# Holding v by whole batch rows: 72 loads of up to nine chunks in place of 144 of one

## The chip, the cores and the metric

The kernel runs on one core of a Trainium2 chip. The metric is the time that the device takes for one execution, in microseconds (us). Runs are compared by their median. Besides the timed runs one execution is recorded by the hardware profiler; it has a time of its own and is the source of every row below.

## What is computed

Three stages follow one another. Attention is done inside chunks of 64 tokens; its output, 4608 rows of 512 numbers, goes through a mixture of eight experts with a skip (a row whose skip score isn't positive passes unchanged, the others go to the expert with the highest logit), and then through a layer that takes the maximum of three products and multiplies it by a fourth matrix. All arrays are float32.

```python
# q, k, v: (8 batches, 8 heads, 576 tokens, 64)
chunk = 64
nc = S // chunk                                   # 9 chunks in a batch
scores = scale * np.matmul(q_c, k_c.transpose(0, 1, 2, 4, 3))
attn = np.exp(scores - np.max(scores, axis=-1, keepdims=True))
attn = attn / (np.sum(attn, axis=-1, keepdims=True) + 1e-09)
x = np.matmul(attn, v_c)                          # then rows of 8 x 64 = 512, token by token
do_compute = x @ w_skip > 0
e_idx = np.argmax(x[do_compute] @ w_gate, axis=1)
y = gate_w[:, None] * (np.maximum(xc @ w1[e], 0.0) @ w2[e])   # for the rows of expert e
h = np.maximum(np.maximum(x @ m2_w1, x @ m2_w2), x @ m2_w3)
out = h @ m2_w_out
```

## The kernel before, in words

The 4608 tokens are walked in 36 tiles of 128 (two chunks each); two tiles make a unit of 256, of which there are 18. A batch has 576 tokens, nine chunks, so units and batches don't end together: `pieces(u)` (L191) gives the parts of a unit that lie in one batch.

`load_qk` (L201) loads q and k of a unit, 512 KB each, in rows of 512 bytes, one transfer for each part. `load_v` (L216) loads v of a unit, one transfer for each chunk and each parity of the heads: 64 tokens stand on 64 partitions (the lower 64 for even heads, the upper 64 for odd ones), four heads of 64 numbers each, so a transfer is 64 KB in pieces of 256 bytes. Eight transfers make a unit and 144 the whole of v. They go into four buffers `v_all` of four chunks each. A column of ones beside each head (L186) makes the matmul of L290 give the row sums too.

All these loads are issued by SP, in the order that the queue of SP has them in. At the start `in_turn` (L575) chains them: q and k of units 0 to 4, with v of units 0, 1 and 2 behind units 1, 2 and 3. Behind those stand two small loads (L590, L591) of the gate's and the skip's weights into `wcat`, 18 KB together. ACT casts `wcat` to `wr` (L592), and DVE writes the other half of `wr` (L593).

Then the loop of L597 runs over the tiles, and PE's instructions stay in the order in which the loop writes them (L596). At step t it does the products with v of tile t-2 (`values`, L283), the scores of tile t (`scores`, L252), the transposes of tile t-1's exponentials, the logits of the unit that ended before (`logits`, L328, the tile `lt` of L333, every second step, for the first time at step 4), the transposes of q and k of the next unit, and the transposes of tile t-2's output. `lt` reads `wr`. At every second step a unit of q and k is loaded ahead (five units) and one of v (three units). Each four tiles make a group; `route` and `place` work out where its rows go, POOL stores the group's rows to `x_dram` (L470) and sends the row numbers (L448).

From step 22 on the first expert's weights are loaded by SP too (L97). The experts start as the last tiles end, and the third stage follows them. None of them reads v.

DMAs that POOL issues are described in a scratch of SBUF; its size is an argument of the constructor (L1132), 16384 bytes of a partition if nothing is said.

Of the kernel before, what the change touches and what calls it, by code (L numbers as in the profile page):

```python
# [9 lines left out]
F32 = mybir.dt.float32  # L10
# [9 lines left out]
P = 128  # L20
B, H, S, D = 8, 8, 576, 64
# [7 lines left out]
NU = N // UT  # L29
# [8 lines left out]
def kernel(  # L38
# [15 lines left out]
    nc = tc.nc  # L54
# [16 lines left out]
    def four_kb(shape, dt, name, aside=False):  # L71
        return bpool.tile(shape, dt, tag="s4" if aside else "b4", name=name, bufs=2 if aside else 4)
# [103 lines left out]
    def two_banks(tag, name):  # L176
        return psum1.tile([P, 2, 512], F32, tag=tag, name=name)

    apool = p1.enter_context(tc.tile_pool(name="apool", bufs=2))
    nc.gpsimd.memset(ids_sb, N)  # L180
    nc.gpsimd.dma_start(ids_dram.rearrange("(p c) o -> p (c o)", p=P), ids_sb)

    NV = 4
    v_all = [apool.tile([P, 4, 4, D + 1], F32, name=f"v_all{i}", bufs=1) for i in range(NV)]
    for i, t in enumerate(v_all):
        (nc.gpsimd if i else nc.vector).memset(t[:, :, :, D], 1.0)  # L186
    none = kpool.tile([1, XW], F32, name="none")
# [3 lines left out]
    def pieces(u):  # L191
        got, t = [], u * UT
        while t < (u + 1) * UT:
            b, s = divmod(t, S)
            n = min((u + 1) * UT - t, S - s)
            got.append((t - u * UT, b, s, n))
            t += n
        return got
# [14 lines left out]
                        dst[pr, h0:h1], src[b, h0:h1, s:s + n, :].rearrange("h (p r) d -> p h (r d)", r=2))  # L213
        units[u] = {"qt": qt, "kt": kt}

    def load_v(u):  # L216
        vb = v_all[u % NV]
        for off, b, s, n in pieces(u):
            for c in range(n // 64):
                for par in range(2):  # L220
                    link["load"] = nc.sync.dma_start(
                        vb[64 * par:64 * par + 64, off // 64 + c, :, :D],
                        v[b, par::2, s + 64 * c:s + 64 * c + 64, :].rearrange("hp k d -> k hp d"),
                    )

    def pair_heads(u, g):
        un = units[u]
        for nm in ("q", "k"):
            r = apool.tile([P, 2, H // 2, D], F32, tag=nm + "r", name=f"{nm}r{u}_{g}", bufs=3)
            (nc.scalar.copy if u == 0 else nc.gpsimd.tensor_copy if nm == "q" and u > 1 else nc.vector.tensor_copy)(  # L230
                r, un[nm + "t"][:, 4 * g:4 * g + 4, :].rearrange("p h (r d) -> p r h d", r=2))
            un[nm + "r", g] = r

    def qk_transpose(u, g):
        un = units[u]
        if g == 0:
            for nm in ("qT", "kT"):
                un[nm] = apool.tile([P, 4, UT], F32, tag=nm, name=f"{nm}{u}")
        for nm in ("q", "k"):
            src, dst = un[nm + "r", g], un[nm + "T"]  # L240
            tr = ps_tr(f"tr{nm}{u}_{g}").rearrange("p (h r t) -> p h r t", h=2, r=2)
            for hh in range(2):
                hp = 2 * g + hh
                for r in range(2):
                    nc.tensor.transpose(
                        tr[:, hh, r, :], src[:, r, 2 * hh:2 * hh + 2, :].rearrange("p h d -> p (h d)"), ident)
            (nc.vector.tensor_copy if nm == "k" and u == 0 else nc.scalar.copy)(
                dst[:, 2 * g:2 * g + 2, :].rearrange("p h (t r) -> p h r t", r=2), tr)
# [23 lines left out]
    def exp_transpose(t):  # L272
# [7 lines left out]
        nc.scalar.copy(aT, tr)  # L280
        un["aT", s] = aT

    def values(t):  # L283
        u, s = divmod(t, 2)
        un = units[u]
        xp = two_banks("xp", f"xp{t}")[:, :, :4 * (D + 1)].rearrange("p r (h d) -> p r h d", h=4)
        for hp in range(4):
            for par, c2 in TILES:
                rows, cols = slice(64 * par, 64 * par + 64), slice(64 * c2, 64 * c2 + 64)
                nc.tensor.matmul(  # L290
                    xp[cols, par, hp, :], un["aT", s][rows, hp, cols], v_all[u % NV][rows, 2 * s + c2, hp, :],
                    start=True, stop=True)
        g, j = PLACE[t]
        if j == 0:
            if g == len(SIZES) - 1:
                parts = [four_kb([P, 1, XW], F32, f"xg{g}_{i}", True) for i in range(SIZES[g])]
            else:
                parts = [bpool.tile([P, GT, XW], F32, tag="xg", name=f"xg{g}")[:, :SIZES[g], :]]
            groups[g] = parts, apool.tile([P, GT, E + 1], F32, tag="lg", name=f"lg{g}")
            for part in parts:  # L300
                nc.gpsimd.memset(part[:, :, DM + 1:], 0.0)
        sm = apool.tile([P, 2, 4], F32, tag="sm", name=f"sm{t}", bufs=3)
        nc.vector.tensor_scalar_add(sm, xp[:, :, :, D], 1e-9)
        nc.vector.reciprocal(sm, sm)
        nc.vector.tensor_tensor(
            rows_of(t)[:, :DM].rearrange("p (h r d) -> p r h d", h=4, r=2), xp[:, :, :, :D],
            sm.unsqueeze(3).to_broadcast([P, 2, 4, D]), op=ALU.mult)

    def rows_of(t):
        g, j = PLACE[t]  # L310
        part, i = divmod(j, groups[g][0][0].shape[1])
        return groups[g][0][part][:, i, :]
# [259 lines left out]
    units, groups, slots, picks, xgs, xT, link, put, sent = {}, {}, {}, {}, {}, {}, {}, {}, []  # L572
    ids_rows = ids_dram.rearrange("(p c) o -> p (c o)", p=P)

    def in_turn(load, u):  # L575
        with tc.issue_after(link["load"].ins) if "load" in link else nullcontext():
            load(u)

    for u in range(5):
        in_turn(load_qk, u)  # L580
        if 0 < u < 4:
            in_turn(load_v, u - 1)
        if u < 2:
            pair_heads(u, 0)
            pair_heads(u, 1)
            if u == 0:
                qk_transpose(0, 0)
                qk_transpose(0, 1)
# [8 lines left out]
    for t in range(NT + LAG):  # L597
        u, s = divmod(t, 2)
        if s == 0 and u + 5 < NU:
            load_qk(u + 5)  # L600
        if u + 2 < NU:
            pair_heads(u + 2, s)
        if t == 8:
            nc.gpsimd.tensor_copy(tok_f, tok_i)
            nc.gpsimd.tensor_scalar_add(tok_f, tok_f, float(-N))
            nc.gpsimd.iota(col_i, pattern=[[1, P]], base=0, channel_multiplier=0)
            nc.gpsimd.tensor_copy(col_f, col_i)
        if 0 <= t - 2 < NT:
            values(t - 2)
        if s == 1 and u + 3 < NU:  # L610
            load_v(u + 3)
        if t < NT:
            scores(t)
        if t % 2 == 0 and 0 <= t - 22 <= 16:
            i = (t - 22) // 2
            with tc.issue_after(link["max"].ins), tc.issue_after(link["exp"].ins):
                if i < 8:
                    with tc.issue_after(link["load"].ins):
                        raws_0[i] = load_raw(*expert_src(0, i))
                if i:  # L620
                    expert_piece(0, i - 1, wpool, raw=raws_0[i - 1])
        if 0 <= t - 1 < NT:
            exp_transpose(t - 1)
        if s == 0 and 0 <= u - 2 < NU:
            logits(u - 2)
        if u + 1 < NU:
            qk_transpose(u + 1, s)
        if 0 <= t - 2 < NT:
            x_transpose(t - 2)
        if s == 1 and 0 <= u - 2 < NU:  # L630
            logits_back(u - 2)
            g, j = PLACE[2 * u - 4]
            if j + 2 == SIZES[g]:
                route(g)
        if s == 0 and 0 <= u - 3 < NU:
            g, j = PLACE[2 * u - 6]
            if j + 2 == SIZES[g]:
                if g == 2:
                    count_first()
                place(g)  # L640
                store_x(g)
                if g == FIRST or START[g] + SIZES[g] == DIRECT:
                    for i in range(max(late[0], t - LAG), START[g + 1]):
                        send_id(i)
                    late = range(START[g + 1], NT - 2)
                if START[g] + SIZES[g] == DIRECT:
                    load_ids(ids_0[:, 2:], ids_rows[:, 2:3])
                if g == FIRST:
                    fill_first(run[(g + 1) % 2][:, 0, 0:1])
                    load_ids(ids_0[:, :2], ids_rows[:, :2])  # L650
                    xgs[0] = [four_kb([P, XW], F32, f"xg_0_{j}") for j in range(2)]
                    rows = START[g + 1] * P
                    at = cpool.tile([P, 2], I32, name="at")
                    nc.vector.tensor_single_scalar(at, ids_0[:, :2], rows - 1, op=ALU.min)
                    for j in range(2):
                        gather(xgs[0][j], at[:, j:j + 1], rows)
        if t - LAG in late:
            send_id(t - LAG)
# [245 lines left out]
    rows = bpool.tile([P, 4, XW], F32, tag="xg", name="xg_0")  # L904
# [243 lines left out]
```

## Time and profile before

| | us |
|---|---|
| median of three runs | 1119.62 |
| lowest and highest of them | 1119.02, 1122.96 |
| the profiled execution | 1127.18 |
| its span, from the first to the last instruction | 1125.4 |
| PE (matmuls) busy | 1024.9 |
| DVE busy | 596.0 |
| ACT busy | 420.8 |
| POOL busy | 326.1 |

The profiled execution is 7.6 us above the median. PE is busy for 91% of the span, though a busy PE needn't be one at its peak. The engines are PE (TensorE), PEld (its weight loads), DVE (VectorE), ACT (ScalarE), POOL (GpSimd) and SP, which issues DMAs; a q behind an engine's name (SPq) stands for its queue. In a row of a timeline the words in brackets say how long the engine had been idle before it and what released it.

### The profile page before, as it was taken

Reading aid. Unit: us, or ns where it says so; the run is one execution under the profiler, and the core shown is the slowest. Engines: PE = TensorE matmul, PEld = TensorE weight load, DVE = VectorE, ACT = ScalarE, POOL = GpSimd, SP = SyncE. Lnnn points to the kernel's source line nnn. Section 1 sums busy time; section 2 is a strip of 40 time slices with the busy share of each in tenths; the row PEclk is TensorE's granted clock in tenths of the full one; section 3 lists DMA queues with packets and bytes.
Section 4 is the critical chain, followed back from the end, with each engine's and each line's share of the span. In section 5 each row is a group of like instructions: output and inputs, shape, how many; then the busy total and the mean of one; then the engine's idle time right before and its main releaser. Section 6 shows DMA issues by size and latency. Waiting matters only on the chain.

```text
span 1125.4 us, 19554 instructions
## 1 busy us (share of the span) xinstructions
PE 1024.9 (91%) x7472; PEld 863.2 (77%) x7472; DVE 596.0 (53%) x1182; ACT 420.8 (37%) x738; POOL 326.1 (29%) x312
## 2 busy tenths in 40 slices
PE   7687787697899997999899799999999999999997
PEld 5576676585897886888688588878887788888996
DVE  3577677746772845642479881444334352443241
ACT  4455465523542524442344342222322242222231
POOL 2123323247431534450233231111311140122121
PEclk8789889999999998999899999999999999999999
DMA  8889975338671827661998935664456644666591
GB/s 204 168 220 211 241 199 160 128 126 316 219 282 67 279 82 263 204 211 39 292 317 297 318 99 171 184 189 147 163 162 186 195 131 143 194 196 203 175 296 38
DMA packets 214769, 217.13 MB, mean 193 GB/s; under 512 B 49931, under 2 KB 178955, under 8 KB 214656
## 3 DMA queue, kind: packets, MB, share of 16 engines
q1 hardware_dynamic: 201472, 174.18, 53.1%
q0 software_dynamic: 10592, 33.20, 8.3%
q10 hardware_dynamic: 2592, 8.26, 1.8%
q8 instruction: 69, 1.13, 0.4%
q14 instruction: 44, 0.36, 0.1%
HBM read 175.15 MB, written 41.83 MB: 193 GB/s over the span
## 4 chain that ended last, share of the span: by engine, by line
PE 44%; DMA 3%; DVE 1%; issue 1%; POOL 1%; ACT 0%; SPq 0%; POOLq 0%; DVEq 0%; ACTq 0%
PE f_a L705 6%; PE f_a L707 6%; PE f_a L706 6%; PE o L705 4%; PE o L707 4%; PE o L706 4%; PE f_d L705 3%; PE f_d L706 3%; PE f_d L707 3%; DMA ws<-m_sums 2%; PE f_b L705 1%; PE f_b L707 1%; PE f_b L706 1%; PE trf L879 1%; DMA m_sums<-n_q 1%
## 5 line engine op out<-in xcount | busy, mean ns | idle before, releaser
L91 POOL TENSOR_TENSOR fh<-best,fh 128x512 fp32r<-128x512 f32 (+1 forms) x60 | 75.0, 1255 | 354.9 <-ACT fh L90 269.5
L705 PE MATMUL f_a<-x_t,ws 128*128 128x512 f32 (+1 forms) x270 | 100.0, 372 | 2.7 <-ACT u L1044 2.7
L707 PE MATMUL f_a<-x_t,ws 128*128 128x512 f32 (+1 forms) x270 | 99.5, 368 | 0.0
L706 PE MATMUL f_a<-x_t,ws 128*128 128x512 f32 (+1 forms) x270 | 99.4, 368 | 0.0
L705 PE MATMUL h<-xhi,whi_e 128*128 128x256 f32 x256 | 76.4, 299 | 13.9 <-ACTq L982 6.4
L90 ACT CAST whi_e<-raw_e 128x1024 fp32r<-128x1024 f32 x64 | 66.5, 1052 | 60.3 <-DMA raw_e<-in_moe_w_dram 28.2
L706 PE MATMUL o<-wlo_m,fh 128*128 128x512 f32 x216 | 84.6, 391 | 0.0
L705 PE MATMUL o<-whi_m,fh 128*128 128x512 f32 x216 | 83.9, 392 | 0.0
L707 PE MATMUL o<-whi_m,fh 128*128 128x512 f32 x216 | 83.3, 392 | 0.0
L706 PE MATMUL h<-xlo,whi_e 128*128 128x256 f32 x256 | 75.8, 297 | 4.6 <-issue 4.6
L705 PE MATMUL y<-whi_e,hhi 128*128 128x512 f32 x184 | 73.6, 402 | 2.1 <-DMA xg<-x_dram,ids_sb 0.8
L707 PE MATMUL h<-xhi,wlo_e 128*128 128x256 f32 x256 | 74.6, 295 | 0.0
L707 PE MATMUL y<-whi_e,hlo 128*128 128x512 f32 x184 | 71.9, 398 | 2.0 <-DVE hlo L773 1.8
L91 POOL TENSOR_TENSOR wlo_e<-raw_e,whi_e 128x1024 fp32r<-128x1024 f32 x21 | 54.2, 2581 | 65.1 <-ACT whi_e L90 64.6
L706 PE MATMUL y<-wlo_e,hhi 128*128 128x512 f32 x184 | 71.8, 393 | 0.0
L91 DVE TENSOR_TENSOR wlo_e<-raw_e,whi_e 128x1024 fp32r<-128x1024 f32 x43 | 59.1, 1383 | 20.7 <-ACT whi_e L90 10.6
L90 ACT CAST fh<-best 128x512 fp32r<-128x512 f32 (+1 forms) x60 | 34.7, 581 | 90.2 <-DVE best L1035 61.3
L705 PEld LDWEIGHTS h<-xhi,whi_e 128*128 128x128 f32 x256 | 52.5, 205 | 17.0 <-ACTq L982 6.8
L705 PEld LDWEIGHTS f_a<-x_t,ws 128*128 128x128 f32 x270 | 51.0, 189 | 12.0 <-ACT u L1044 3.5
L1038 ACT COPY p<-f_a 128x512 f32<-128x512 f32 (+1 forms) x45 | 24.4, 546 | 91.7 <-PE f_a L707 91.5
L706 PEld LDWEIGHTS f_a<-x_t,ws 128*128 128x128 f32 x270 | 51.0, 189 | 8.4
L707 PEld LDWEIGHTS f_a<-x_t,ws 128*128 128x128 f32 x270 | 50.9, 189 | 8.5
(226 smaller groups left out, 2592.1 us busy)
## 6 DMA issues: line engine op xcount, KB each, us to landing
ws<-m_sums SPq DMA_DIRECT2D x135, 512.0 KB
raw_e<-in_moe_w_dram SPq DMA_DIRECT2D x64, 512.0 KB
ws<-m_sums SPq DMA_DIRECT2D x45, 256.0 KB
v_all<-in_v_dram SPq DMA_DIRECT2D x144, 64.0 KB
x<-x_dram SPq DMA_DIRECT2D x36, 256.0 KB
out_dram<-os SPq DMA_DIRECT2D x36, 256.0 KB
x_dram<-xg POOLq DMA_DIRECT2D x8, 1040.0 KB
m_sums<-n_raw ACTq DMA_DIRECT2D x18, 448.0 KB
```

Of the source, the lines that this page charges most:

```text
L90: nc.scalar.copy(hi, src),
L91: eng.tensor_tensor(lo, src, hi.bitcast(F32), op=ALU.subtract),
L705: nc.tensor.matmul(acc, ahi, bhi, start=first, stop=False, skip_group_check=onto)
L706: nc.tensor.matmul(acc, ahi, blo, start=False, stop=False, skip_group_check=onto)
L707: return nc.tensor.matmul(acc, alo, bhi, start=False, stop=last, skip_group_check=onto)
L879: nc.tensor.transpose(tr[:, i * P:(i + 1) * P], row[:, c * P:(c + 1) * P], ident)
L1038: nc.scalar.copy(p1, acc_a)
```

## The change

`v_all` becomes three buffers of nine chunks, one for each batch that is held. `load_v(b, c0, c1)` loads chunks c0 to c1 of a batch, one transfer for each of the eight heads, so a whole batch is eight transfers of 147,456 bytes, still to 64 partitions and in pieces of 256 bytes. At the start batch 0 is loaded in two parts, of four and of five chunks, behind units 1 and 2, and batches 1 and 2 behind units 3 and 4. In the loop the next batch is loaded once the last tile that reads the oldest one has been passed. `values` takes each chunk from the buffer of its batch. The scratch of POOL's DMAs is set to 8192 bytes.

```diff
-    NV = 4
-    v_all = [apool.tile([P, 4, 4, D + 1], F32, name=f"v_all{i}", bufs=1) for i in range(NV)]
+    NV, CB = 3, S // 64
+    v_all = [apool.tile([P, CB, 4, D + 1], F32, name=f"v_all{i}", bufs=1) for i in range(NV)]
...
-    def load_v(u):
-        vb = v_all[u % NV]
-        for off, b, s, n in pieces(u):
-            for c in range(n // 64):
-                for par in range(2):
-                    link["load"] = nc.sync.dma_start(
-                        vb[64 * par:64 * par + 64, off // 64 + c, :, :D],
-                        v[b, par::2, s + 64 * c:s + 64 * c + 64, :].rearrange("hp k d -> k hp d"),
-                    )
+    def load_v(b, c0=0, c1=CB):
+        for h in range(H):
+            rows = slice(64 * (h % 2), 64 * (h % 2) + 64)
+            link["load"] = nc.sync.dma_start(
+                v_all[b % NV][rows, c0:c1, h // 2, :D],
+                v[b, h, 64 * c0:64 * c1, :].rearrange("(c k) d -> k c d", k=64))
...
+    def v_of(chunk):
+        return v_all[chunk // CB % NV][:, chunk % CB]
...
-                    xp[cols, par, hp, :], un["aT", s][rows, hp, cols], v_all[u % NV][rows, 2 * s + c2, hp, :],
+                    xp[cols, par, hp, :], un["aT", s][rows, hp, cols], v_of(2 * t + c2)[rows, hp, :],
...
+    first_v = {1: [(0, 0, 4)], 2: [(0, 4, CB)], 3: [(1,)], 4: [(2,)]}
     for u in range(5):
         in_turn(load_qk, u)
-        if 0 < u < 4:
-            in_turn(load_v, u - 1)
+        for part in first_v.get(u, ()):
+            in_turn(load_v, *part)
...
-        if s == 1 and u + 3 < NU:
-            load_v(u + 3)
+        done = (2 * t - 2) // CB - 1
+        if done >= 0 and (2 * t - 4) // CB <= done and done + NV < B:
+            load_v(done + NV)
...
-    nc = _bacc.Bacc("TRN2", target_bir_lowering=False, num_devices=1)
+    nc = _bacc.Bacc("TRN2", target_bir_lowering=False, num_devices=1, dynamic_dma_scratch_size=8192)
```

SP's queue at the start, from the second load of v to the two loads of `wcat`, before (the number behind q, k and v_all is the unit or the buffer; sizes are partitions x pieces x numbers):

```order
L221 DMA v_all1_142<-in_v_dram 64x4x64 x8
L212 DMA qkt3_235<-in_q_dram 128x8x128
L212 DMA qkt3_235<-in_k_dram 128x8x128
L221 DMA v_all2_143<-in_v_dram 64x4x64 x8
L212 DMA qkt4_246<-in_q_dram 64x8x128
L212 DMA qkt4_246<-in_k_dram 64x8x128
L212 DMA qkt4_246<-in_q_dram 64x8x128
L212 DMA qkt4_246<-in_k_dram 64x8x128
L590 DMA wcat_99<-in_moe_w_gate_dram 128x4x8
L591 DMA wcat_99<-in_moe_w_skip_dram 128x4x1
```

The same stretch of SP's queue in the changed kernel:

```order
L219 DMA v_all0_141<-in_v_dram 64x5x64 x8
L212 DMA qkt3_233<-in_q_dram 128x8x128
L212 DMA qkt3_233<-in_k_dram 128x8x128
L219 DMA v_all1_142<-in_v_dram 64x9x64 x8
L212 DMA qkt4_244<-in_q_dram 64x8x128
L212 DMA qkt4_244<-in_k_dram 64x8x128
L212 DMA qkt4_244<-in_q_dram 64x8x128
L212 DMA qkt4_244<-in_k_dram 64x8x128
L219 DMA v_all2_143<-in_v_dram 64x9x64 x8
L591 DMA wcat_99<-in_moe_w_gate_dram 128x4x8
L592 DMA wcat_99<-in_moe_w_skip_dram 128x4x1
```

The transfers of v have five and nine chunks in place of four, and a third set of eight stands between unit 4 and `wcat`. In both kernels the first load of v, eight transfers of 64 KB into `v_all0`, stands ahead of this stretch.

DVE around the output of tile 1 (`xg0`, the first group's rows) and the copies of unit 3's k (`kr3`), before:

```order
L304 RECIPROCAL sm1_461<-sm1_461 128x8
L230 COPY kr3_0_362<-qkt3_235 128x512
L230 COPY kr3_1_442<-qkt3_235 128x512
L305 TENSOR_TENSOR xg0_381<-xp1_444,sm1_461 128x2x4x64
L264 TENSOR_REDUCE mx3_490<-sc3_473 128x8
```

The same place in the changed kernel:

```order
L304 RECIPROCAL sm1_459<-sm1_459 128x8
L305 TENSOR_TENSOR xg0_379<-xp1_442,sm1_459 128x2x4x64
L227 COPY kr3_0_360<-qkt3_233 128x512
L227 COPY kr3_1_440<-qkt3_233 128x512
L261 TENSOR_REDUCE mx3_480<-sc3_463 128x8
```

The output of tile 1 has moved ahead of the two copies of k. The products on PE stand in the order of before; only the buffer that they take v from differs.

## Rows read from the trace of the kernel before

**Rows 1.** Two stretches: start and end; busy us (instructions) by engine, PE clock, DMA share, GB/s.
```profile
0.00:226.00 226.00, 172.14 (x3116) 143.91 (x3117) 147.93 (x456) 119.07 (x235) 63.52 (x107) 0.88 0.78 192
226.00:1125.00 899.00, 852.74 (x4359) 719.25 (x4356) 448.11 (x727) 301.71 (x503) 262.60 (x206) 0.98 0.60 193
```

**Rows 2.** Timeline of DVE, maxima of tiles 5, 9, 21, 25 and 33: start, us.
```profile
47.04 0.68 DVE L264 TENSOR_REDUCE mx<-sc 128x8 f32<-128x512 f32 x1
...
66.06 0.68 DVE L264 TENSOR_REDUCE mx<-sc 128x8 f32<-128x512 f32 x1
...
133.22 0.68 DVE L264 TENSOR_REDUCE mx<-sc 128x8 f32<-128x512 f32 x1
...
157.63 0.63 DVE L264 TENSOR_REDUCE mx<-sc 128x8 f32<-128x512 f32 x1
...
203.18 0.64 DVE L264 TENSOR_REDUCE mx<-sc 128x8 f32<-128x512 f32 x1
```

**Rows 3.** Two stretches of the steady part, columns as in rows 1.
```profile
66.00:133.00 67.00, 55.43 (x1040) 47.05 (x1039) 46.38 (x152) 35.67 (x76) 22.00 (x31) 0.90 0.93 222
158.00:203.00 45.00, 35.92 (x693) 29.89 (x691) 34.16 (x106) 27.57 (x54) 15.76 (x21) 0.92 0.51 151
```

**Rows 4.** Waits of PE up to 230 us: us in total, times, longest.
```profile
PE sc L260 <- issue: 11.5, 26, 1.1
...
PE lt L333 <- DVE wr L593: 7.4, 1, 7.4
```

**Rows 5.** Timelines of PE, ACT and DVE around the wait for `wr`.
```profile
40.24 1.04 PE L333 MATMUL lt<-xh,wr 128*18 128x256 f32 x4 [7.37 <-DVE wr L593]
...
39.73 0.22 ACT L592 CAST wr<-wcat 128x36 fp32r<-128x36 f32 x1 [5.01 <-DMA wcat<-in_moe_w_skip_dram]
...
39.34 0.43 DVE L230 COPY kr<-qkt 128x512 f32<-128x512 f32 x1 [5.28 <-DMA qkt<-in_k_dram]
39.99 0.20 DVE L593 TENSOR_TENSOR wr<-wcat,wr 128x36 fp32r<-128x36 f32 x1 [0.22 <-ACT wr L592]
```

**Rows 6.** Timeline of SP's queue: start, us taken by the issues.
```profile
2.94 0.51 SPq L212 DMA_DIRECT2D qt<-in_q_dram  x1
...
5.49 6.76 SPq L221 DMA_DIRECT2D v_all<-in_v_dram  x8
...
14.50 6.69 SPq L221 DMA_DIRECT2D v_all<-in_v_dram  x8
...
32.01 0.62 SPq L590 DMA_DIRECT2D wcat<-in_moe_w_gate_dram  x1
```

**Rows 7.** Short stretches of the start, columns as in rows 1.
```profile
2.00:8.00 6.00, 4.61 (x23) 3.50 (x23) 0.69 (x1) 2.78 (x7) 3.79 (x18) 1.00 0.97 282
...
11.00:13.00 2.00, 2.00 (x20) 1.52 (x12) 1.34 (x3) 0.62 (x1) 0.00 (x0) 0.50 0.63 114
20.00:22.00 2.00, 0.89 (x7) 0.44 (x5) 1.26 (x5) 1.08 (x3) 0.00 (x0) 1.00 0.42 81
27.00:29.00 2.00, 0.00 (x0) 0.00 (x0) 1.24 (x3) 0.09 (x1) 0.05 (x1) 0.95 0.83 136
29.00:31.00 2.00, 1.74 (x31) 1.44 (x34) 1.41 (x3) 0.61 (x2) 0.00 (x0) 0.50 0.43 88
41.50:43.50 2.00, 2.00 (x11) 1.93 (x10) 0.00 (x0) 0.84 (x2) 0.38 (x1) 0.50 0.89 163
```

**Rows 8.** The tile `v_all`: issues, ns min/median/max; who waited for it, us, times.
```profile
L221 SPq DMA_DIRECT2D v_all<-in_v_dram x144: 324/607/3697, 5.5 to 180.8; - x144
...
PEld xp L290: 2.9, 3
```

**Rows 9.** The stretch of the lower clock after the wait, columns as in rows 1.
```profile
35.60:45.90 10.30, 5.66 (x68) 4.88 (x72) 1.55 (x4) 2.45 (x5) 1.23 (x2) 0.50 0.82 171
```

**Rows 10.** Timeline of PE, the transposes of tile 1's output.
```profile
29.26 1.09 PE L318 MATMUL trx<-ident,xg 128*128 128x128 f32 x4 [2.83 <-DVE xg L305]
```

**Rows 11.** DMA queue of POOL on the page: packets, MB, share of 16 engines.
```profile
q0 software_dynamic: 10592, 33.20, 8.3%
```

More of the change, by code (lines that the diff above doesn't have):

```diff
@@ L573, with in_turn @@
     ids_rows = ids_dram.rearrange("(p c) o -> p (c o)", p=P)
-    def in_turn(load, u):
+    def in_turn(load, *what):
         with tc.issue_after(link["load"].ins) if "load" in link else nullcontext():
-            load(u)
+            load(*what)
+    first_v = {1: [(0, 0, 4)], 2: [(0, 4, CB)], 3: [(1,)], 4: [(2,)]}
     for u in range(5):
         in_turn(load_qk, u)
-        if 0 < u < 4:
-            in_turn(load_v, u - 1)
+        for part in first_v.get(u, ()):
+            in_turn(load_v, *part)
         if u < 2:
```

## Prediction

> **What bounds the kernel now.** I read the views from the outside in: the whole span in two stretches, the pace of the attention tiles, the waits of TensorE, then the one long wait step by step back to its DMA. The change touches only attention's loads. In the attention stage, the first 226 us, TensorE (PE) is busy 172 us and the DMA engines 78% of the time; in the other 899 us PE is busy 853 us and no `v` is loaded [rows 1]. So only the first stretch can move by itself; what comes later starts when it ends.
>
> Is that stretch bound by loads? The DVE's maximum over a tile's scores comes once a tile, so its starts are a clock; the 36 of them are counted from tile 0. From tile 9 to tile 21 there are 67.16 us, or 5.60 a tile; from tile 25 to tile 33, 45.55 us, or 5.69 a tile [rows 2]. In the first of these stretches the DMA engines are 93% busy, in the second 51% [rows 3]. The pace is the same, so in the steady part loads don't set it. The start is different: among PE's waits one is 7.4 us long, before `lt` of L333, for `wr` of L593 [rows 4]. Its chain: PE stands until 40.24, DVE writes `wr` at 39.99, ACT casts it at 39.73 after 5.0 us of waiting for the `wcat` DMA; just before, at 39.34, DVE got the `k` rows of unit 4 [rows 5]. So at 39.7 us everything stands for the smallest load of the kernel, 18 KB, because SP issues it behind five units of `q` and `k` and three of `v`: at 32.0 [rows 6]. PE, ACT and DVE each take their instructions in order, so all three stand.
>
> **The change, part by part.** *What stands ahead of `wcat`.* Before: 24 transfers of `v`, 12 chunks of 64 tokens. Now: 8 of four chunks, 8 of five, 16 of nine, which is 27 chunks in 32 transfers; `q` and `k` ahead of it are the same. A chunk is 64 tokens x 8 heads x 64 numbers x 4 B = 131,072 B, so 15 chunks more are 1.966 MB. How fast they move is not in the trace for this shape. Where loads of `v` were queued in the DMA engines behind others, 2 us moved 163 GB/s at a share of 0.89; from there 1.966 MB take 12.1 us. The fastest stretch, `q` and `k` alone, is 282 GB/s: 7.0 us. The slowest, where `v` trickled in as SP issued it, is 81 GB/s: 24.3 us [rows 7]. I take 163, since it is `v` itself, queued, and larger transfers are queued.
>
> One thing is given back. An issue of 64 KB holds SP for a median of 0.607 us [rows 8], eight with their gaps 6.7 us [rows 6], so while `v` was issued the DMA engines ran dry: shares of 0.63, 0.42, 0.83 and 0.43 in four pieces of 2 us, 3.4 us of idling together [rows 7]. A nine-chunk transfer is 147,456 B, 0.90 us at 163 GB/s, more than its issue, so the engines stay fed. The four-chunk part is as before (its 0.74 us stays), the five-chunk part keeps some 0.4: 2.2 us come back. `wcat` lands 12.1 - 2.2 = **9.9 us later**, and PE's wait of 7.4 us becomes some 17. A check without a rate: eight more issues of 0.607 us make 4.9 us, so even if the size of a transfer cost nothing, `wcat` could not come as early as before.
>
> The trace's 163 GB/s and a rule of the Trainium skill stand side by side here, in "SBUF — State Buffer", section "Door 1: The DMA port swizzle": a transfer to 64 partitions reaches only half of the SBUF's ports, and 196 GB/s was measured at 1 MiB. By that rule, as an estimate, the 1.966 MB would take 10.0 us instead of 12.1 and the sum below would be 2.1 us smaller, 1126.0; the trace's rate is below the page's, and no row here shows a large load to 64 partitions by itself.
>
> *Whether the delay is passed on.* Work from `lt` on stands in the same order. After the wait the tiles ran at 4.76 us (19.02 us from tile 5 to tile 9) [rows 2], and the list of PE's waits that [rows 4] are from, 23 entries up to 230 us, names no DMA. I see no slack that would swallow it: pass on all of it. The clock after the wait was 1.2 GHz for 10 us [rows 9]; a longer wait needn't make that stretch longer, 0, with 2.8 us either way as bounds (half of the 5.7 us of work it held).
>
> *What is saved.* PE's weight loads waited three times for `v` landings, 2.9 us in all [rows 8]; with three batches held ahead these go. Not all of it reached the tiles after; I take half, -1.4, with 0 and -2.9 as bounds. SP issues 72 transfers instead of 144 (batch 0 in two parts, so 8 more than 64): 44 us of SP's time by the median. Nobody waits for that later on, 0; if loads did set the pace, that is the second rival. The reloads sit behind the last use of a batch, in SP's queue ahead of the next units' `q` and `k`: the reload into the first buffer follows unit 9, and its first reader is nine tiles after the release, some 50 us at 5.6, so it is hidden. The DVE's order shifts by two copies: the one that writes `x` of tile 1 now stands before the copies that wait for unit 3. The 2.83 us that PE waited there [rows 10] may go, but it lies before the wait for `wcat`, which would grow by the same: 0. Fewer and wider memsets: off every path, 0.
>
> *Half the scratch.* It holds the descriptors of POOL's DMAs, 8.3% of the DMA time [rows 11]. No row shows POOL waiting for room, so a gain is excluded. POOL is busy 63.5 of the 226 us [rows 1]; if the smaller room made that a tenth more, 6 us, its 162 us of idling would hide them. I take 0; 6 us is the bound, if all of it fell on stores that others wait for.
>
> **Sum:** +9.9 - 1.4 = **+8.5 us**. The profiled execution took 1127.18 us (span 1125.4), 7.6 above the median of the three runs; it would become 1135.7. On the median, 1119.62 + 8.5 = **1128.1 us**.
>
> **The rivals.** *1, the delay is mostly swallowed, no change.* If the extra `v` moves at the 282 GB/s bound the wait grows by 7.0 - 2.2 = 4.8, and all 2.9 of the waits for `v` come back: +1.9, 1121.5 us. For it: more rows are in SBUF when PE starts again. Against: 163 GB/s for queued `v`.
>
> *2, faster: SP's issues were the bound.* It decides if the steady tiles are late because loads are. Then 26 tiles after tile 9 would run at 4.76 instead of 5.60, 21.8 us less: 1128.1 - 21.8 = 1106.3. Against: the same pace at DMA shares of 0.93 and 0.51, and PE's 11.5 us before the scores that are put down to "issue" rather than a DMA [rows 3, 4]. The Trainium skill, "DMA: Bandwidth & Descriptors", section "Rules for kernel authors", is on this rival's side: many small transfers should be made into few large ones. By that rule the loads get cheaper, and the trace agrees that 64 KB issues leave the engines half idle; it does not agree that the tiles wait for them.
>
> *3, much slower: a long transfer is paced like a short one.* If an issue's time grows with its bytes, or nine chunks to 64 partitions crowd each other, `v` goes on moving at 81 GB/s: +24.3 - 1.4, 1142.5 us. Against: SP took 6.7 us for 8 x 64 KB but issued 512 KB of `q` in 0.51 us [rows 6], so bytes don't pace it.
>
> That the change doesn't do what it says I give nothing: the order of the changed kernel shows the 16 nine-chunk loads ahead of `wcat`.
>
> **How the numbers follow.** Forecast 0.52, own range 1123 to 1134; rival 1 0.23, rival 2 0.13, rival 3 0.12. A measurement here can tell 0.5%, 5.6 us, from no change: the borders are 1114.0 and 1125.2. Slower: 0.48 of the forecast's case and rival 3, 0.60. Same: rival 1 and 0.04, 0.27. Faster: 0.13. The range leaves out most of rival 2 and the upper part of rival 3: 1114 to 1139.
>
> **What would show it.** Right: PE's wait before `lt` grows from 7.4 to about 17 us and ends near 50 us; ACT's wait for `wcat` with it; the DMA share while nine-chunk `v` is moved is near 1; tiles 9 to 33 keep 5.6 to 5.7 us; attention ends some 8 us later and the rest takes 899 us as before. Wrong step by step: `wcat` landing before 45 us means that the rate was above my 163; a pace clearly under 5.6 us means that loads did matter; a wait before the second stage that shrinks by the same amount means that the delay is not passed on. The forecast is wrong if PE starts `lt` by 42 us.

## The result, and the profile after

| | before, us | after, us | ratio, 95% interval |
|---|---|---|---|
| first comparison (8 and 8 runs) | 1119.65 | 1126.38 | 1.0058 (1.0033 to 1.0082) |
| again, second chip (16 and 6) | 1126.25 | 1135.38 | 1.0102 (1.0071 to 1.0133) |
| again, third chip (17 and 6) | 1127.00 | 1136.67 | 1.0093 (1.0061 to 1.0125) |

The changed kernel is slower, by 6.7 to 9.7 us in the medians. The forecast was +8.5 us and 1128.1; the median of the first comparison is 1126.38.

The first trace of the changed kernel is of an execution of 1120.63 us, the shortest of its eight, and the trace of before was of one of 1127.18, above all eight timed ones (1117.05 to 1122.96). Those two don't make a pair, so both kernels were traced again, twice, each time both on one chip. First the trace that came with the result; the two stretches, columns as in [rows 1]:

```profile
0.00:226.00 226.00, 164.75 (x3141) 138.75 (x3142) 148.43 (x472) 120.19 (x238) 68.05 (x110) 0.89 0.87 194
226.00:1118.00 892.00, 848.67 (x4333) 715.03 (x4331) 445.57 (x710) 300.15 (x500) 254.66 (x202) 0.98 0.61 194
```

The waits of PE up to 235 us in the same trace, answering to [rows 4]:

```profile
PE lt L333 <- DVE wr L594: 15.8, 1, 15.8
...
PE sc L257 <- issue: 2.9, 2, 1.6
```

The wait before `lt` has doubled, as forecast (about 17). Its chain, in the timelines of PE, ACT and DVE, is that of [rows 5], later:

```profile
47.49 1.04 PE L333 MATMUL lt<-xh,wr 128*18 128x256 f32 x4 [15.82 <-DVE wr L594]
...
46.98 0.22 ACT L593 CAST wr<-wcat 128x36 fp32r<-128x36 f32 x1 [13.53 <-DMA wcat<-in_moe_w_skip_dram]
...
40.54 0.43 DVE L227 COPY kr<-qkt 128x512 f32<-128x512 f32 x1 [7.75 <-DMA qkt<-in_k_dram]
47.23 0.20 DVE L594 TENSOR_TENSOR wr<-wcat,wr 128x36 fp32r<-128x36 f32 x1 [6.27 <-ACT wr L593]
```

`k` of unit 4 lands 1.2 us later than before (39.34), `wcat` 7.25 us later (39.73). Between the two, SP's queue in this trace, answering to [rows 6], shows why: two sets of eight nine-chunk loads.

```profile
22.41 8.37 SPq L219 DMA_DIRECT2D v_all<-in_v_dram  x8
...
33.72 9.13 SPq L219 DMA_DIRECT2D v_all<-in_v_dram  x8
42.89 0.63 SPq L591 DMA_DIRECT2D wcat<-in_moe_w_gate_dram  x1
```

Now the pair from the third chip. The waits of PE up to 235 us, before:

```profile
PE sc L260 <- issue: 11.5, 22, 1.1
...
PE lt L333 <- DVE wr L593: 7.6, 1, 7.6
```

and after:

```profile
PE lt L333 <- DVE wr L594: 17.0, 1, 17.0
PE sc L257 <- issue: 11.7, 25, 1.1
```

The timelines of ACT (the cast of `wcat`) and DVE (the maxima of tiles 5, 9 and 35), before:

```profile
39.46 0.22 ACT L592 CAST wr<-wcat 128x36 fp32r<-128x36 f32 x1 [4.70 <-DMA wcat<-in_moe_w_skip_dram]
...
46.77 0.68 DVE L264 TENSOR_REDUCE mx<-sc 128x8 f32<-128x512 f32 x1
...
65.87 0.68 DVE L264 TENSOR_REDUCE mx<-sc 128x8 f32<-128x512 f32 x1
...
214.07 0.68 DVE L264 TENSOR_REDUCE mx<-sc 128x8 f32<-128x512 f32 x1
```

and after:

```profile
48.71 0.22 ACT L593 CAST wr<-wcat 128x36 fp32r<-128x36 f32 x1 [14.28 <-DMA wcat<-in_moe_w_skip_dram]
...
55.68 0.68 DVE L261 TENSOR_REDUCE mx<-sc 128x8 f32<-128x512 f32 x1
...
74.67 0.68 DVE L261 TENSOR_REDUCE mx<-sc 128x8 f32<-128x512 f32 x1
...
222.94 0.68 DVE L261 TENSOR_REDUCE mx<-sc 128x8 f32<-128x512 f32 x1
```

The cast of `wcat` is 9.25 us later, tile 5 8.91, tile 9 8.80, tile 35 8.87; the spans are 1125.0 and 1135.2. In the pair from the second chip it is 9.74 for the cast (38.55 and 48.29), 9.62 for tile 9 and 10.77 for tile 35. So in matched traces the delay comes into being in one wait and is carried to the end of attention.

In the first trace of after it is not. There tile 9 is at 72.91 us, 6.85 behind the first trace of before, tile 21 at 133.20, level with it, and tile 35 at 209.14 against 214.02. One difference is in the other row shown: PE's waits inside the scores that are put down to "issue" (stalls, from here on) are 2.9 us there, 11.5 in the first trace of before, and 11.5 and 11.7 in the pair. The experiments had to tell whether this belongs to the change.

### The profile page after: what moved, and what is told of

Read it like the earlier page. It is cut to its first block, busy times and chain, and to the rows that moved or that the text cites. A ratio compares the mean times of both kernels' runs of the same rounds, so it can differ in the third digit from the quotient of the medians.

```text
span 1118.9 us, 19430 instructions
## 1 busy us (share of the span) xinstructions
PE 1013.4 (91%) x7472; PEld 853.8 (76%) x7472; DVE 594.0 (53%) x1182; ACT 420.3 (38%) x738; POOL 322.7 (29%) x311
## 4 chain that ended last, share of the span: by engine, by line
PE 43%; DMA 6%; DVE 2%; issue 1%; POOL 0%; ACT 0%; SPq 0%; POOLq 0%; DVEq 0%; ACTq 0%
PE f_a L707 5%; PE f_a L709 5%; PE f_a L708 5%; PE o L707 4%; PE o L708 4%; PE o L709 4%; PE f_d L707 3%; DMA ws<-m_sums 3%; PE f_d L709 3%; PE f_d L708 3%; PE f_b L707 1%; PE f_b L709 1%; PE f_b L708 1%; DMA m_sums<-n_q 1%; PE trf L881 1%
## 5 line engine op out<-in xcount | busy, mean ns | idle before, releaser
L91 DVE TENSOR_TENSOR wlo_e<-raw_e,whi_e 128x1024 fp32r<-128x1024 f32 x43 | 56.4, 1320 | 23.2 <-ACT whi_e L90 21.4
```

The costliest lines, as they stand in the source:

```text
L91: eng.tensor_tensor(lo, src, hi.bitcast(F32), op=ALU.subtract),
```

## The experiments

**Both kernels once more.** No edit; the runs are `b_again` and `a_again` on the second chip.

> The kernel before once more, for a second trace: the first was of an execution 7.6 us above the median. If the steady pace that was read there (5.60 us a tile from tile 9 to tile 21) is the usual one, this trace shows it again within 0.1 us, and so does the wait before the logits, 7.4 us. If the first trace was of an unusually slow execution, the tiles 9 to 21 take some 5.0 us each here and the attention stage ends some 7 us earlier than at 226 us.

> The changed kernel once more, for a second trace and a tighter interval. The first trace (an execution 5.8 us under the median) has the wait before the logits at 15.8 us instead of 7.4, and gives it back between tile 9 and tile 35. If the giving back belongs to the change, it is here too (tiles 9 to 21 at 5.0 us). If it is luck of one execution, tiles 9 to 21 take some 5.5 us here while the wait is again 15.8 us within 1. Time against before: 0.3 to 0.8% slower by either.

The steady pace of before was there again: 67.21 us from tile 9 to tile 21, 5.60 a tile. The changed kernel took 68.82 there, 5.73 a tile, not 5.0; its wait before the logits was 17.0. So the giving back of the first trace doesn't belong to the change alone. The stalls in the scores are 11.1 and 12.6 us in these two.

**The small load early.** In the changed kernel `wcat` is loaded behind unit 1.

```diff
     for u in range(5):
         in_turn(load_qk, u)
+        if u == 1:
+            in_turn(load_wcat)
...
-    with tc.issue_after(link["load"].ins):
-        nc.sync.dma_start(wcat[:, :, :E], w_gate.rearrange("(c p) e -> p c e", p=P))
-        nc.sync.dma_start(wcat[:, :, E], w_skip.rearrange("(c p) -> p c", p=P))
```

> The changed kernel with the 18 KB of gate and skip weights loaded behind unit 1 instead of behind all v. Theory 1, the later landing of these weights is what the change costs: the wait for them is gone, the next thing waited for is k of unit 4, at 41 us by the changed kernel's trace (40.5), so some 6 us come back: 1118 to 1121. Theory 2, the cost lies elsewhere (the half scratch, long transfers that crowd other DMAs later): the time stays at 1124 to 1128 although the wait is gone.

Measured: 1131.58, ratio 1.0051 (1.0023 to 1.0080), where the changed kernel had 1.0102 on the same chip: half came back. The trace splits this. At tile 9 nearly all is back: 66.15 us, against 74.60 in `a_again` and 64.98 in `b_again`. From tile 9 to tile 15 it then takes 41.70 us, where the two others take 36.0 and 35.5. DVE's maxima of tiles 9 and 15 in this kernel:

```profile
66.15 0.68 DVE L261 TENSOR_REDUCE mx<-sc 128x8 f32<-128x512 f32 x1
...
107.85 0.68 DVE L261 TENSOR_REDUCE mx<-sc 128x8 f32<-128x512 f32 x1
```

ACT's timeline shows one cause that isn't in the loads: the earlier `wcat` changed the order that the scheduler gives ACT.

```profile
85.05 0.23 ACT L358 ACTIVATE rex<-rdl 128x32 f32<-128x32 f32 x1 [1.00 <-DVE rdl L356]
85.19 0.57 ACT L277 COPY aT<-trp 128x512 f32<-128x512 f32 x1
88.71 0.63 ACT L266 ACTIVATE ex<-ex 128x512 f32<-128x512 f32 x1 [2.95 <-DVE ex L263]
89.24 0.34 ACT L335 COPY lgT<-lt 18x256 f32<-18x256 f32 x1
```

The exponential stands ahead of `lgT` and of the copies of `q` and `k` behind it, so they wait 2.95 us for something that they don't need. A second one is in the DMAs: POOL, before it clears the buffer for the next group's rows, waits 5.62 us at 92.81 for the store of an earlier group to land (in `a_again` it waits 0.5 us for such stores in all of attention). Theory 1 expected some 6 us back; 3.8 came back in the medians and 5.8 at tile 35 (217.56 against 223.34). It was right about the wait; what the other order and the late store cost each was not told apart.

**Batches 1 and 2 of v behind the small load.**

```diff
-    first_v = {1: [(0, 0, 4)], 2: [(0, 4, CB)], 3: [(1,)], 4: [(2,)]}
+    first_v = {1: [(0, 0, 4)], 2: [(0, 4, CB)]}
...
         nc.sync.dma_start(wcat[:, :, E], w_skip.rearrange("(c p) -> p c", p=P))
+    in_turn(load_v, 1)
+    in_turn(load_v, 2)
```

> The changed kernel with batches 1 and 2 of v loaded behind the gate and skip weights: 9 chunks of v stand ahead of them, where the kernel before had 12 and the changed one 27. Theory 1: the weights land at some 37 us, 3 us earlier than in the kernel before and 10 earlier than in the changed one, and the time goes to 1115 to 1119, if batch 1 lands in time (it is needed for tile 4, some 10 us later). Theory 2: 1124 to 1128.

The weights were cast at 36.36 us (expected 37), 11.9 earlier than in `a_again`. The time was 1132.72, 1.0071 (1.0046 to 1.0096): 0.2% under the changed kernel's 1135.38, where theory 1 had 0.6 to 1.0. The 2.36 MB of batches 1 and 2 now stand ahead of units 5 to 9: DVE waits 6.5 us for `k` and POOL 18.4 us for `q` between 45 and 66 us, and tile 9 is at 68.19. So what stands behind a large load comes late, whichever load that is. Part of this run's time has another cause again: POOL waits 6.5 us for the stores of the groups' rows, as in `a_wcat_early`.

**The old schedule with the new buffers and transfers.** Batch buffers, transfers by head and the half scratch stay; `v` is loaded by units.

```diff
-        done = (2 * t - 2) // CB - 1
-        if done >= 0 and (2 * t - 4) // CB <= done and done + NV < B:
-            load_v(done + NV)
+        if s == 1 and u + 3 < NU:
+            load_v_of(u + 3)
...
+    def load_v_of(u):
+        for c in range(4 * u, 4 * u + 4):
+            if c == 4 * u or c % CB == 0:
+                load_v(c // CB, c % CB, min(c % CB + 4 * u + 4 - c, CB))
```

> The changed kernel, its three buffers, its transfers by head and its half scratch, but v loaded unit by unit (four chunks) at the places where the kernel before loads it, so that 12 chunks stand ahead of the gate and skip weights and not 27. Theory 1, the 15 chunks of v that are loaded too early cost the time, wherever the wait for them shows: within 0.3% of the kernel before, and the weights land within 1 us of it. Theory 2, the form of the transfers or the scratch costs it: 0.5 to 1.0% slower than before.

1149.48 us, 1.0303 (1.0261 to 1.0344): neither theory had room for it. A unit that spans two batches takes 16 transfers, so there are 192 and not 144. At the start this makes 32 transfers ahead of `wcat` in place of 24, for the same 12 chunks, and the cast comes at 44.07 us, 5.06 later than in `b_scratch` (39.01, same chip), where within 1 us was expected. That is the prediction's check without a rate, eight more issues of 0.607 us or 4.9 us, seen by itself. The tile `v_all` (ns of an issue: least, median, most), and the timelines of SP's queue and of ACT:

```profile
L219 SPq DMA_DIRECT2D v_all<-in_v_dram x192: 465/601/2338, 5.8 to 202.9; - x192
```

```profile
151.78 13.28 SPq L219 DMA_DIRECT2D v_all<-in_v_dram  x16
...
166.37 1.33 SPq L97 DMA_DIRECT2D raw_e<-in_moe_w_dram  x1
...
172.78 1.04 ACT L90 CAST whi_e<-raw_e 128x1024 fp32r<-128x1024 f32 x1 [19.87 <-DMA raw_e<-in_moe_w_dram]
```

48 more issues at the median of 0.601 us are 28.8 us of SP. Tile 35 came at 236.43 us, 27.9 later than in `b_scratch`. That the two numbers are so near is partly chance, for the delay has two parts: 6.3 us are there at tile 9 and still at tile 24, and 19.2 come in one step at tile 25, where ACT stands 19.87 us for the first expert's weights, which SP issues only at 166.37, and everything behind ACT stands with it. This was the theory that the prediction had put among its rivals at another place: SP's queue can hold attention, by a load far down in it.

**The scratch alone.** The kernel before with `dynamic_dma_scratch_size=8192`; no instruction moves on SP, ACT or DVE.

> The kernel before with the scratch of 8192 bytes alone; no instruction moves. Theory 1: no change, within 0.25%. Theory 2 with the scratch as cause: 0.3 to 1.0% slower.

1119.73, 1.0019 (0.9988 to 1.0050): no cost can be told. The interval reaches to 5.6 us, nearly the prediction's bound of 6, but not to the change's cost on the second and third chips.

**The small load later, in the kernel before.** `wcat` behind units 5 and 6 of q and k and unit 3 of v.

```diff
-    with tc.issue_after(link["load"].ins):
-        nc.sync.dma_start(wcat[:, :, :E], w_gate.rearrange("(c p) e -> p c e", p=P))
...
             load_qk(u + 5)
+        if t == 2:
+            with tc.issue_after(link["load"].ins):
+                nc.sync.dma_start(wcat[:, :, :E], w_gate.rearrange("(c p) e -> p c e", p=P))
```

> The kernel before with the two loads of the gate and skip weights moved behind units 5 and 6 of q and k and unit 3 of v (2.62 MB): the same bytes in nearly the same order, only these 18 KB later, by some 12 to 14 us at 190 to 220 GB/s. If the wait for them is what costs, as the prediction has it, it is passed on in full and the time is 1.0 to 1.3% above the kernel before. If it is the amount of v loaded early that costs, the other loads go on during the wait, the tiles after it are faster, and the time is 0 to 0.5% above.

The cast came at 51.54 us, 12.5 later than in `b_scratch` (39.01) on the same chip, and tile 5 12.8 later. The time was 1121.20, 1.0038 (1.0011 to 1.0065): 3.7 us in the medians, so two thirds were given back. So the time fell where the second theory had it, and the tiles after the wait were faster, as it said. No trace of this chip has the stalls in the scores to speak of (0 to 4.5 us), and without them attention meets other DMAs. Two waits of DVE show where the delay went: for the stores of the groups' rows (`x_dram`), whose buffers the next groups reuse, and for the row numbers (`ids`) that the first expert's rows are fetched by. DVE's wait for the stores in total, its maxima of tiles 9, 30 and 35, and its wait for the row numbers, in `b_scratch`:

```profile
DVE xg L305 <- DMA x_dram<-xg: 8.4, 4, 3.3
...
65.05 0.68 DVE L264 TENSOR_REDUCE mx<-sc 128x8 f32<-128x512 f32 x1
...
178.08 0.68 DVE L264 TENSOR_REDUCE mx<-sc 128x8 f32<-128x512 f32 x1
...
185.63 0.17 DVE L654 TENSOR_SCALAR at<-ids 128x2 int32<-128x2 int32 x1 [5.70 <-DMA ids<-ids_dram]
...
208.54 0.68 DVE L264 TENSOR_REDUCE mx<-sc 128x8 f32<-128x512 f32 x1
```

and in `b_wcat_late`, where DVE doesn't wait for the stores at all:

```profile
79.07 0.68 DVE L264 TENSOR_REDUCE mx<-sc 128x8 f32<-128x512 f32 x1
...
183.68 0.68 DVE L264 TENSOR_REDUCE mx<-sc 128x8 f32<-128x512 f32 x1
...
187.98 0.17 DVE L655 TENSOR_SCALAR at<-ids 128x2 int32<-128x2 int32 x1 [2.90 <-DMA ids<-ids_dram]
...
213.38 0.68 DVE L264 TENSOR_REDUCE mx<-sc 128x8 f32<-128x512 f32 x1
```

The delay is 14.0 us at tile 9 and 5.6 at tile 30, 8.4 less, as much as DVE waits for the stores in `b_scratch`. The wait for the row numbers takes 2.8 more, and at tile 35 the delay is 4.84. In the pair from the third chip DVE waits 1.4 us for the stores in the kernel before and none in the changed one, and 0.7 us for the row numbers in both, and there the delay is passed on. So "passed on in full" holds where nothing further on waits for a DMA anyway; where something does, that wait takes a part of it. The first trace of after, put beside `b_scratch`, fits for the most part: it is 7.9 us late at tile 9 and 0.6 at tile 35, and its two waits, 5.1 and 3.36 us, are 3.3 and 2.3 shorter.

Two reservations. The orders of ACT, DVE and POOL in `b_wcat_late` aren't those of `b_scratch` (PE's is), and the store of the second group's rows stands elsewhere on POOL. And `b_scratch`, which has half the scratch, stands in here for the kernel before, of which this chip gave no trace. Six traces are without the stalls or nearly so: the three of kernels with half the scratch (`b_scratch`, `a_by_unit` and the first of after) have 4.0 to 8.4 us of DVE's waits for the stores, the three of kernels with all of it 0 to 1.2. Whether the scratch has a part in those waits is open.

**The small load early, in the kernel before.** `wcat` behind unit 1, as above.

> The kernel before with these two loads behind unit 1 of q and k. By the trace of before k of unit 4 lands 0.4 us ahead of them, so the wait only goes to another tile: within 0.3% of the kernel before by every theory that has the start bound by the bytes loaded. If the wait before the logits itself were the cost (6 to 7 us, as predicted), 0.4 to 0.6% faster.

1115.27, 0.9983 (0.9959 to 1.0006): no difference that can be told. Tile 9 came at 63.67, 1.4 us before that of `b_scratch`: `k` of unit 4 is next, as expected. Tile 23 came at 132.43, 7.8 before it (DVE's waits for the stores are 1.2 us here and 8.4 there), and tile 35 at 208.37, level; the trace is of the longest of this kernel's twelve executions. SP's queue, ACT and DVE show where the lead went:

```profile
136.05 3.32 SPq L221 DMA_DIRECT2D v_all<-in_v_dram  x4
139.42 0.59 SPq L97 DMA_DIRECT2D raw_e<-in_moe_w_dram  x1
...
171.50 7.84 SPq L221 DMA_DIRECT2D v_all<-in_v_dram  x8
179.43 1.07 SPq L97 DMA_DIRECT2D raw_e<-in_moe_w_dram  x2
180.82 0.34 SPq L464 DMA_DIRECT2D ids<-ids_dram  x1
...
145.98 1.04 ACT L90 CAST whi_e<-raw_e 128x1024 fp32r<-128x1024 f32 x1 [6.82 <-DMA raw_e<-in_moe_w_dram]
...
185.11 0.17 DVE L657 TENSOR_SCALAR at<-ids 128x2 int32<-128x2 int32 x1 [7.95 <-DMA ids<-ids_dram]
```

The first expert's weights are issued at 139.42 behind the `v` of late units, and the read of the row numbers at 180.82 behind eight loads of `v` and two of weights, though POOL had issued the last of the stores that it reads at 174.10. Each makes a tile 12 us long (tiles 25 and 31).

**Both kernels a third time, and the changed kernel with both costs taken away.** `b_third` and `a_third` have no edit. `a_late_v` has `wcat` behind unit 1 as in `a_wcat_early`, only batch 0 of `v` at the start, and:

```diff
+    first_step = {0: 1, 5: 2, 9: 3, 15: 4, 19: 5, 23: 6, 27: 7}
...
-        done = (2 * t - 2) // CB - 1
-        if done >= 0 and (2 * t - 4) // CB <= done and done + NV < B:
-            load_v(done + NV)
+        if t in first_step:
+            load_v(first_step[t])
```

> The kernel before, for a trace from the same chip as the next two. Two kinds of execution have shown: with stalls of PE inside the scores put down to issue (11 to 13 us in the attention stage: both traces of before, the second of the changed kernel), and nearly without (0 to 4.5 us). With stalls I expect the maximum of tile 35 at 212 to 214 us. Without, the loads that SP issues late hold tile 31 (as in the kernel before with half the scratch, 10 us there) and tile 35 comes at 208 to 209, no earlier however early the logits of tile 4 are.

> The changed kernel on that chip. Theory 1, the wait before the logits is passed on in full in any execution: 10 us later than before at tile 35 and 0.8 to 1.0% slower. Theory 3, it is passed on only where SP's queue doesn't hold the kernel before anyway: with the stalls in the scores 10 us later (tile 35 at 222 to 224, 0.9 to 1.0% slower); without them before waits some 10 us at tile 31 for SP and the changed kernel doesn't, so tile 35 within 2 us of it and 0 to 0.3% slower.

> The changed kernel with both costs of the start taken away: the gate and skip weights behind unit 1, and each batch of v from the second on loaded some six steps before its first reader (steps 0, 5, 9, 15, 19, 23, 27) and not as soon as there is a buffer; 72 issues of v as in the changed kernel. If the amount of v loaded early is what delays q and k, and SP's queue is what holds the kernel before at tiles 25 and 31, this one has neither: tile 9 by 64 us (66.2 with the weights early alone), no wait for the expert's weights at tiles 25 and 31, tile 35 at 198 to 206 us, and 0.5 to 1.2% faster than before. If only the wait before the logits counts, it is at the kernel before, within 0.4%.

The pair is the one shown above: stalls in both (11.5 and 11.7 us), tile 35 at 214.07 and 222.94, ratio 1.0093. Theory 1 and theory 3 give the same here; the case that tells them apart, the changed kernel on a chip without the stalls, didn't come up. `a_late_v` missed its mark: 1131.41, 1.0042 (1.0018 to 1.0066), with tile 9 at 64.52 as expected, but 74.65 us from tile 9 to tile 21, where before took 67.32, and tile 35 at 219.74 in place of 198 to 206. ACT has the same changed order as in `a_wcat_early`, with the same 2.95 us. POOL waits 7.45 us for the store of a group's rows to end before it clears the buffer, 2.2 in `b_third`. So it is no clean trial of its loads, and whether the changed kernel gains by them is open.

**SP's queue put right, in the kernel before.** On top of `b_wcat_early`; ACT's and DVE's orders are those of `b_wcat_early`.

```diff
-        if t % 2 == 0 and 0 <= t - 22 <= 16:
-            i = (t - 22) // 2
+        if t % 2 == 0 and 0 <= t - 20 <= 18:
+            i = (t - 20) // 2
...
-                if i:
-                    expert_piece(0, i - 1, wpool, raw=raws_0[i - 1])
+                if i > 1:
+                    expert_piece(0, i - 2, wpool, raw=raws_0[i - 2])
...
-                    load_ids(ids_0[:, :2], ids_rows[:, :2])
+                    load_ids(ids_0[:, :2], ids_rows[:, :2], nc.gpsimd)
```

> The kernel before with the gate and skip weights behind unit 1 (as in b_wcat_early), the first expert's weights loaded two tiles earlier, and the first row numbers read back by POOL's queue and not SP's. No instruction of ACT or DVE moves against b_wcat_early, where PE came to tile 23 at 132.4 us and then waited 12 us at tile 25 for the first expert's weights and 12 us at tile 31 for the row numbers, both issued late by SP. Theory 3, SP's queue is what holds the kernel before there: both waits shrink to 6 us together or less, tile 35 at 194 to 202 us, and 0.6 to 1.4% faster than before where PE has no stalls in the scores; with those stalls (11 to 13 us) PE comes later, SP holds nothing, and it is 0.2 to 0.6% faster. If SP's queue isn't the cause, tile 35 stays at 208 and the time at that of b_wcat_early (0 to 0.4% faster).

1108.59 us, 0.9885 (0.9853 to 0.9918): 1.15% faster than the kernel before, on a chip whose trace has no stalls in the scores (0.2 us). SP's queue, POOL and DVE:

```profile
128.68 0.60 SPq L97 DMA_DIRECT2D raw_e<-in_moe_w_dram  x1
...
169.31 0.59 POOL L464 DMA_DIRECT2D ids<-ids_dram  x1 [2.14 <-DMA ids_dram<-tok_i,rslot]
...
171.38 0.17 DVE L657 TENSOR_SCALAR at<-ids 128x2 int32<-128x2 int32 x1 [2.80 <-DMA ids<-ids_dram]
...
193.71 0.68 DVE L264 TENSOR_REDUCE mx<-sc 128x8 f32<-128x512 f32 x1
```

The weights are issued 10.7 us earlier, ACT waits for none of them in a tile, the row numbers wait for their own stores alone, and tile 35 comes at 193.71, 14.7 us before that of `b_wcat_early`; the spans are 1105.3 and 1119.6, 14.3 apart (the two traces are from different chips, and that of `b_wcat_early` is of its longest execution; the ratio is against before on the same chip). This is the fastest version of the study, and it keeps the 144 loads of `v`. Three edits were made at once, and their shares weren't measured by themselves. On a chip with the stalls it wasn't tried.

## Why the prediction was right, and where it was not

*The wait for `wcat`.* Right in place, cause and size. Forecast: landing 9.9 us later, wait about 17 us, ended near 50. In the matched pairs 9.25 and 9.74 later, wait 17.0 in both, ended at 49.22 and 48.80. That the load's place is the cause is shown from both sides: in `a_wcat_early`, with `wcat` early and all 27 chunks still ahead of unit 5, tile 9 is 8.45 us earlier than in the changed kernel and 1.2 later than in the kernel before; in `b_wcat_late`, with `wcat` late and `v` loaded as in the kernel before, tile 5 is 12.8 us later.

*The rate.* Right as well. I took 163 GB/s. Two stretches of the changed kernel in `a_third` while the second set of nine-chunk loads is moved, the first with `q` and `k` of unit 4 in it, the second after DVE has copied that `k` (at 41.74):

```profile
34.00:43.00 9.00, 0.00 (x0) 0.00 (x0) 0.43 (x1) 0.43 (x1) 0.61 (x1) 0.50 1.26 186
...
42.00:46.00 4.00, 0.00 (x0) 0.00 (x0) 0.17 (x1) 0.00 (x0) 0.00 (x0) 0.50 1.35 169
```

In the second every piece that moves is under 512 bytes, so it is `v` by itself, at 169 GB/s; `a_again` has 172 in the same stretch. At 170 the 1.966 MB are 11.6 us, and less the 2.2 given back the term is 9.4, where 9.25 and 9.74 were measured; the 2.2 by itself no run shows. The 196 GB/s that the Trainium skill gives in "SBUF — State Buffer", section "Door 1: The DMA port swizzle", for a transfer of 1 MiB to 64 partitions would make it 10.0 us in place of 11.6, as an estimate. The measurement, with loads of 147 KB in pieces of 256 bytes, is lower than the page's figure, and it decides. Rival 3, long transfers at 81 GB/s, is out. One argument against it was wrong, though: an issue of nine chunks did take longer, eight of them 9.13 us against 6.7 for eight of four [rows 6]. It goes with full DMA engines (share 1.26 here); whether the size of the transfer has a part in it was not tried apart.

*The -1.4 for the waits for v.* Right that they go (`PEld xp` waits 2.5 us for `v` in `b_third`, of them 1.7 near 154 us, and none in `a_third`), wrong that half would reach the end: from tile 9 to tile 35 it is 148.20 and 148.27 us in that pair. The term is 0; measured without it, 9.25 at the cast and 8.87 at tile 35. In the sum of 8.5 this is the term that was mis-sized.

*Passed on, clock, scratch, rest.* Right in the matched pairs. Tiles 5 to 9 take 19.10 and 18.99 us in the pair, so nothing was given back there and the clock after the wait cost nothing more than before. From tile 35 to the end it is 910.9 and 912.3. The scratch is within its interval of 0. That work from `lt` on stands in the same order is so for PE; on ACT, DVE and POOL a few instructions changed places (DVE's routing of the second group, POOL's store of it), which those times don't show. The restriction is where the stalls are absent: most of a delay can be swallowed there, as `b_wcat_late` shows. That outcome is rival 1's, its mechanism isn't: it is not faster loads of `v` but DVE's waits for stores and row numbers. That my list of PE's waits named no DMA didn't exclude them: in `b_scratch` it has PE waiting for `xg` of DVE, 8.2 us between 65 and 180 us, and there DVE waits for the stores.

*SP's 44 us, costed at nothing.* This step failed for the executions without the stalls, in the kernel before at least. I wrote that nobody waits for SP later on. That came from one trace, of an execution with the stalls, where it is true. It costs the forecast nothing in the pairs, which have them; that they have them is luck. `a_by_unit` shows the price of SP's time: 48 more issues, 27.9 us at tile 35. And `b_wcat_early` shows who waits: ACT for the first weights, DVE for the row numbers. My evidence against rival 2 was the same pace at DMA shares of 0.93 and 0.51 [rows 3], read where the stalls add to both; and a share tells of the DMA engines, not of how long a small load stands in SP's queue. The rule of the Trainium skill that I put on that rival's side ("DMA: Bandwidth & Descriptors", "Rules for kernel authors": many small transfers into few large ones) agrees with `a_by_unit`, where more transfers of the same bytes cost 3%. The change itself follows the rule and is slower all the same, because the few large ones were also put ahead of a small one that three engines wait for.

What stays open: the first comparison gave +0.58%, and its trace, of the shortest of its eight runs and nearly without the stalls, ends attention only 0.6 us after `b_scratch`, a trace of the kernel before's order without them, on another chip. Whether the longer seven had the stalls isn't known. The timed runs hint at it: the kernel before takes 1126.25 and 1127.00 us on the two chips whose traces have the stalls, 1117.55 and 1121.64 on the two whose traces don't, and 1119.65 in the first comparison. If that one was without them, the change costs 0.58% there, more than the 0 to 0.3% expected for `a_third` in that case; no run shows it. How much the saved SP time is worth to the changed kernel where there are no stalls wasn't measured beside the kernel before.

## What to carry to other kernels

SP issued its loads here in the order of its queue: before you fill a queue with bulk, find the smallest load in it that an in-order engine waits for, and put that one first. The same reading, done with it for the loads at the end of the stage, was worth 1.15% here, where the change cost 0.6 to 1.0%. Look at a second execution of the same kernel before you read a steady pace from one. When the list of an engine's waits names no DMA, look at what the engines that it waits for wait for. And when you move a load, compare the scheduler's order on the engines that you didn't mean to touch.

## What was not expected of the hardware

In some executions PE stands inside the scores, every four or so products, for 0.4 us or more, and the profile shows nothing that it waits for. It does so while POOL issues the four DMAs of row numbers (L448) and for about 1 us behind the last of them (in `a_third` also beside two gathers that POOL issues at 197 and 199 us, L479). PE and POOL in `b_third`:

```profile
68.26 0.34 PE L260 MATMUL sc<-kT,qT 64*64 64x64 f32 x4 [0.40 <-issue]
69.00 0.36 PE L260 MATMUL sc<-kT,qT 64*64 64x64 f32 x5 [0.40 <-issue]
...
66.78 0.99 POOL L448 DMA_INDIRECT ids_dram<-tok_i,rslot  x1 [0.30 <-issue]
68.08 0.98 POOL L448 DMA_INDIRECT ids_dram<-tok_i,rslot  x1 [0.31 <-issue]
```

All seven traces from two of the chips show it, in both kernels and in three variants of the changed one, 10.7 to 12.6 us in attention; so does the first trace of before, 11.5. The five traces from the two other chips have 0 to 4.5 us with the same DMAs on POOL, and the first trace of after 2.9. So the kernel doesn't decide it, and hardly the scratch (`b_scratch` hasn't the stalls, the changed kernel with the same scratch has them). What it is was not settled. It matters for the reading: it hides waits that an execution without it has.
